# A parallel H3 convolution and ReLU FFN on one core: operand preparation in single steps, matmuls of the first classical product by high parts, a second half staged in row buffers, PSUM seeded by ScalarE, and longer pauses ahead of two convolution stages

## The chip, the cores and the metric

The kernel runs on one core of a Trainium2 chip. The time is device time in microseconds of one execution, median of several. The profile is of one further execution; its span runs from the first to the last instruction of the core.

## The reference

For `S = 2048` tokens and `D = 576` channels, with `xn` the rows of `x = A_q` after layer normalization:

```
k_shift = causal depthwise convolution of k with 4 taps (shift_k)
kv      = k_shift * v
y       = causal convolution of kv with ssm_k, over all 2048 positions, per channel   (FFT)
y       = y + kv * ssm_D
A       = xn * y
B       = relu(xn @ w1) @ w2           # w1: 576 x 4608, w2: 4608 x 576
out     = x + A + B
```

All is float32.

## The kernel before, in words

**FFN.** A float32 factor is split into a high part (rounded to fp32r) and a low part (the rest), and a product is three matmuls: high by high, high by low, low by high. The tokens are handled in two halves of 1024, the 4608 hidden units in 18 chunks of 256. A half with a chunk is a *quad*, `g` from 0 to 35. In a quad two token blocks `b` of 512 and two column blocks `f` of 128 make a 2 by 2 product. Quads 0 and 1 do it with four *classical* products (`classical`, 14 matmuls of 512 columns each). Quads 2 to 35 (`quad`) do it with seven products (`product`, six matmuls each) on the combined operands `00, 01, s2, s1, s3, s4, 11` and combined weights `wa, wb, wc, wd`, and four short `rest` products (`hl`, `wr`) for the last 64 of the 576 channels. The hidden sums stand in two PSUM banks that are used in turn (`psh`, tags h0 and h1). `hidden` ends a sum: ScalarE writes its ReLU as high part `hh`, VectorE the rest as low part `ll`, and only then is the bank free.

Between the products of quad `g` stand the eight *units* of quad `g - 1` (`mm2`: 12 matmuls of 288 columns, for 128 tokens): hidden units times `w2`, summed in a tile `pso` of PSUM, of which there are two. VectorE adds `pso` to the row tile `acc` (L656; L652 in the quads 0 and 1, with `rstd` as factor), which frees it. `split_w` splits weights, high parts on ScalarE (L444), low parts on GpSimd (L445), and GpSimd also issues the loads of the weights.

**Start.** Quads 0 and 1 work on centred rows that are not yet scaled by `rstd`. For quad 2 the scaled operands of blocks 0 and 1 are made by `scales` (a diagonal of `rstd`, `diag`, times a tile of ones on TensorE gives a row of factors, copied by ScalarE), `scaled` (VectorE multiplies `xf`), `combined` (differences for s1 to s4), `made` and `made_rest` (splits). The bottom of the function writes the calls in their order. The operands of the second half are made later, in `later_operands`: rows loaded, normalized, stored, transposed, combined, split into a tile `stg`, and stored to `ops_n`, from which quads 17 on load them.

**Convolution.** `conv` is a generator with the stages fb (`later_operands`), fk (first transform of the filter, `ks` and `zk`), fx (taps `tap`, `gate`, split `xs`, first transform `zx`), fm (`spectrum`, `product_of`, `way_back`) and fo (inverse transform, gate with `xn`, sum with the FFN). Each stage has its own tile pool, and the pools take over each other's memory. `tick(cost)` runs after each FFN piece, adds the piece's matmul columns to a clock, and draws the next step of `conv` when the clock times `rate` has paid for the weights (`W_FK`, `W_FX`, ...) of the steps drawn. A step that yields `-n * PAUSE` (16000 columns) stops the drawing until so many FFN columns have been issued: that is the lead time between a stage's loads and its first use. What a stage posts on VectorE and ScalarE stands behind the last `acc` and `hh` posted before it (`here`).

The order on each engine is then set by a list scheduler at build time (a model of the engines, which may move an instruction that depends on nothing ahead of or behind its place in the program). Each engine works through its list in order. SP issues the loads of `k`, `v`, `zt` and the rows, and the stores, in one queue; the loads of the weights and of the transform matrices stand in GpSimd's.

## Time and profile before

| | |
|---|---|
| time, median of 3 runs | 1096.8 us (1094.36 to 1098.38) |
| profiled execution | 1097.09 us, span 1095.0 us |
| TensorE (PE) busy | 1051.7 us, 96% |
| VectorE (DVE) busy | 769.9 us, 70% |
| ScalarE (ACT) busy | 485.5 us, 44% |
| GpSimd (POOL) busy | 457.8 us, 42% |
| granted TensorE clock, mean | 0.991 |

PE is the engine that is nearly always busy, so what can change the time is where it waits, and where its clock is lowered. The stages follow from the tiles at work: quads 0 and 1 to 62 us, quad 2 from 69 us, fb to about 285 us, fk to 425 us, fx to 700 us, fm from 743 to 975 us, fo to 1075 us.

### The profile page before, as it was taken

The page shows a single profiled execution, that of the slowest core. Times are in us where ns is not written, and L with a number is a line of the kernel's source. Part 1 is how long each engine was busy: PE and PEld are TensorE (multiplying, and loading weights), DVE is VectorE, ACT ScalarE, POOL GpSimd, SP SyncE. Part 2 cuts the span into 40 slices and gives each one's busy share as a digit, 9 for nine tenths or more (in the row PEclk, how much of TensorE's full clock was granted, in tenths as well). Part 3 has the DMA queues.
Part 4 walks back from the last instruction along what each step waited for, and adds up shares of the span by engine and source line. Part 5 has one row for each costly group of instructions (what it writes and reads, how often), then busy time and mean ns, then how long its engine had stood idle before and what let it go on. Part 6 is the DMA issues. An engine that isn't in the chain of part 4 may idle for free. (4 is left out here: it accounts for less than half of the span.)

```text
span 1095.0 us, 17070 instructions
## 1 busy us (share of the span) xinstructions
PE 1051.7 (96%) x6300; PEld 870.8 (80%) x6300; DVE 769.9 (70%) x1149; ACT 485.5 (44%) x929; POOL 457.8 (42%) x496
## 2 busy tenths in 40 slices
PE   8878999999999999798999999999999999999998
PEld 5766899999899998697899899895666665677777
DVE  5787768554887774999999999853444454446765
ACT  7342344333687774344444445434444444432220
POOL 3343454444354444454444445443223223244450
PEclk9989999999999999999999999999999999999999
DMA  6118544992254445589944433237566666457684
GB/s 166 58 38 187 144 150 183 197 154 56 89 160 139 140 140 160 153 259 349 279 134 138 137 114 120 78 138 194 174 197 208 189 209 203 131 179 223 220 248 119
DMA packets 118431, 179.45 MB, mean 164 GB/s; under 512 B 66381, under 2 KB 67551, under 8 KB 116556
## 3 DMA queue, kind: packets, MB, share of 16 engines
q1 hardware_dynamic: 99212, 121.99, 39.3%
q0 software_dynamic: 18816, 55.49, 17.0%
q10 hardware_dynamic: 320, 0.88, 0.3%
q8 instruction: 50, 0.82, 0.3%
q14 instruction: 33, 0.27, 0.1%
HBM read 123.27 MB, written 45.61 MB: 154 GB/s over the span
## 5 line engine op out<-in xcount | busy, mean ns | idle before, releaser
L501 PE MATMUL pso<-w,hh 128*128 128x288 f32 x2304 | 471.4, 297 | 5.4 <-DVE acc L652 3.3
L501 PEld LDWEIGHTS pso<-w,hh 128*128 128x128 f32 x2304 | 381.1, 189 | 36.2 <-issue 8.2
L501 PE MATMUL pso<-w,ll 128*128 128x288 f32 x1152 | 340.4, 295 | 0.0
L656 DVE TENSOR_TENSOR acc<-pso,acc 128x576 f32<-128x576 f32 x272 | 204.6, 753 | 158.0 <-PE pso L501 156.7
L501 PEld LDWEIGHTS pso<-w,ll 128*128 128x128 f32 x1152 | 217.1, 188 | 0.0
L445 POOL TENSOR_TENSOR w<-r,w 128x576 fp32r<-128x576 f32 x72 | 111.5, 1552 | 134.6 <-ACT w L444 134.5
L445 POOL TENSOR_TENSOR wb<-sums,wb 128x512 fp32r<-128x512 f32 x34 | 49.8, 1465 | 203.8 <-ACT wb L444 140.9
L501 PE MATMUL psh<-x,wa 128*128 128x512 f32 x408 | 109.0, 402 | 10.8 <-DVE ll L522 6.5
L501 PE MATMUL psh<-xs,wb 128*128 128x512 f32 x408 | 108.7, 400 | 1.2 <-ACT u L581 1.2
L501 PEld LDWEIGHTS psh<-x,wa 128*128 128x128 f32 x408 | 74.7, 190 | 32.6 <-issue 12.7
L501 PEld LDWEIGHTS psh<-xs,wb 128*128 128x128 f32 x408 | 72.9, 189 | 25.0 <-issue 11.7
L501 PE MATMUL psh<-hl,wr 128*128 128x512 f32 x272 | 88.1, 401 | 1.5 <-ACT psh L604 1.5
L521 ACT ACTIVATE hh<-psh 128x512 fp32r<-128x512 f32 x68 | 40.6, 598 | 91.0 <-PE psh L501 90.7
L604 ACT ACTIVATE psh<-psh 128x512 f32<-128x512 f32 x34 | 19.9, 584 | 132.7 <-DVE u L602 132.7
L445 POOL TENSOR_TENSOR wd<-r,wd 128x256 fp32r<-128x256 f32 x36 | 31.7, 881 | 97.1 <-ACT wd L444 97.1
L522 DVE SCALAR_TENSOR_TENSOR ll<-psh,hh 128x512 fp32r<-128x512 f32 x68 | 46.6, 685 | 34.1 <-ACT hh L521 33.7
L868 DVE TENSOR_TENSOR k<-psf,k 128x512 f32<-128x512 f32 x72 | 44.7, 682 | 36.5 <-PE psf L687 31.6
L676 DVE TENSOR_TENSOR ks<-kt,ks 64x288 fp32r<-64x288 f32 x64 | 54.5, 852 | 18.1 <-ACT ks L675 17.0
L445 POOL TENSOR_TENSOR wa<-r,wa 128x512 fp32r<-128x512 f32 x36 | 51.5, 1430 | 28.8 <-ACT wa L444 28.7
L501 PEld LDWEIGHTS psh<-hl,wr 128*128 128x128 f32 x272 | 46.9, 188 | 19.2 <-issue 12.3
L521 ACT ACTIVATE hh<-p 128x512 fp32r<-128x512 f32 x34 | 21.5, 632 | 90.4 <-DVE p L611 65.4
L501 PE MATMUL psh<-xs,wc 128*128 128x512 f32 x204 | 53.3, 396 | 8.1 <-DVE ll L522 8.1
(146 smaller groups left out, 1642.8 us busy)
## 6 DMA issues: line engine op xcount, KB each, us to landing
r<-in_w POOLq DMA_DIRECT2D x70, 288.0 KB, 3.5
r<-in_w POOLq DMA_DIRECT2D x35, 512.0 KB, 5.2
zk<-zk SPq DMA_DIRECT2D x32, 288.0 KB, 2.6
zx<-zx SPq DMA_DIRECT2D x32, 288.0 KB, 2.7
ztk<-zk SPq DMA_DIRECT2D x18, 512.0 KB, 3.9
ztx<-zx SPq DMA_DIRECT2D x18, 512.0 KB, 3.9
k<-k SPq DMA_DIRECT2D x72, 128.0 KB, 3.2
zy<-vo SPq DMA_DIRECT2D x18, 512.0 KB, 2.6
```

Of the source, the lines that this page charges most:

```text
L445: nc.gpsimd.tensor_tensor(w[:, 1, :n], src, w[:, 0, :n], OP.subtract)
L501: last = nc.tensor.matmul(ps, a, m, start=start and n == 0, stop=n == len(seq) - 1, skip_group_check=True)
L521: done["act"] = nc.scalar.activation(hh, ps, AF.Relu)
L522: nc.vector.scalar_tensor_tensor(ll, ps, 0.0, hh, op0=OP.max, op1=OP.subtract)
L604: nc.scalar.activation(x, y, AF.Copy, scale=-1.0)
L656: done["acc"] = nc.vector.tensor_tensor(two(acc[t]), ps[:, :, :NH], two(acc[t]), OP.add)
L676: nc.vector.tensor_tensor(dst[other], src[own], dst[own], OP.subtract)
L868: nc.vector.tensor_tensor(filt[n][c][:, k, :], banks[k], filt[n][c][:, k, :], OP.mult)
```

## The change

It changes these parts (names as in the code; a `PAUSE` is 16000 columns):

- `classical`: with `g == f == 0` the eight matmuls on the operands' high parts stand first, the four on their low parts after them. Before, high and low parts alternated.
- The start: both diagonals are made before the units; `scales(1)` and `scales(0)` have matmuls between them and the diagonals. The operands of quad 2 are made by a generator, `second_half_of_start`, one chunk a step; `post` draws steps after units and classical products, `need` draws until an operand that is asked for is ready. Units and products of quad 1 stand in another order, quad 2 is issued within the pool `fa`, and the convolution begins with quad 3.
- `quad`: unit 3 stands ahead of the product with s1, and unit 4 ahead of the product with s3; before, they stood behind these.
- Seeds: while `stage["seeded"]` is (3, 4), which is from the opening of the pool of fx to that of fm, units 3 and 4 have ScalarE copy `acc` into `pso` (`open_unit`), the matmuls add to it, and ScalarE copies `pso` back to `acc`. VectorE's sum falls away for them. There are 26 such units.
- `later_operands`: all four row tiles are loaded at once (four buffers, before three), and the tile `stg` is replaced by the row buffers, with two stores of 512 KB an operand instead of one of 1 MB.
- The four loads of `sk` move from SP's queue to GpSimd's.
- Pacing: the pause between the loads and the first step of fx is 4 (before 2.5), the steps up to its first transform pause 2.375 (before 1.125); in fm the pause is 3.5 (before 1.5). `KT_GAP`, `PAUSES`, `SHARE`, `FFN_TOTAL` and the weights `W_...` take other values.

Three places show how instructions move. VectorE, from the first low part of operand 00 (`x00`) to the end of the third sum of quad 1 (`ll1_1_0`), whose bank takes the first product of quad 2; before:

```order
L207 TENSOR_TENSOR x00_622<-xf00_227,x00_622 128x512 x2
L207 TENSOR_TENSOR x01_627<-xf01_229,x01_627 128x512 x2
L203 TENSOR_TENSOR hl0_632<-xfr0_231,hl0_632 64x512
L457 TENSOR_TENSOR sums2_662<-r1_2_420 128x256 x2
L221 TENSOR_TENSOR xf10_335<-xf10_335,xf00_227 128x512 x2
L207 TENSOR_TENSOR xs1_567<-xfs1_564,xs1_567 128x512
L313 TENSOR_TENSOR xfr1_339<-xfr1_339,row1_558 64x512
L207 TENSOR_TENSOR xs1_567<-xfs1_564,xs1_567 128x512
L207 TENSOR_TENSOR xs2_635<-xfs2_619,xs2_635 128x512 x2
L522 SCALAR_TENSOR_TENSOR ll1_1_0_656<-psh1_c10_640,hh1_1_0_655 128x512
```

and now:

```order
L207 TENSOR_TENSOR x00_614<-xf00_227,x00_614 128x512 x2
L221 TENSOR_TENSOR xfs2_646<-xf00_227,xfs1_583 128x512
L508 TENSOR_TENSOR sums2_651<-r1_2_420 128x256 x2
L221 TENSOR_TENSOR xfs2_646<-xf00_227,xfs1_583 128x512
L508 TENSOR_TENSOR sums2_651<-sums2_651,r1_2_420 128x256
L575 SCALAR_TENSOR_TENSOR ll1_1_0_635<-psh1_c10_619,hh1_1_0_634 128x512
```

Twelve operations stood between; now five do, two of them the combination of s2, which stood ahead of `x00` before. The rest now stands behind `ll1_1_0`.

VectorE, the making of block 1's rest operand `hl1`, which the `rest` behind unit 6 of quad 1 reads in quad 2; before:

```order
L522 SCALAR_TENSOR_TENSOR ll1_1_1_686<-psh1_c11_670,hh1_1_1_685 128x512
L207 TENSOR_TENSOR x11_713<-xf11_337,x11_713 128x512 x2
L207 TENSOR_TENSOR xs3_701<-xf10_335,xs3_701 128x512 x2
L203 TENSOR_TENSOR hl1_719<-xfr1_339,hl1_719 64x512
L207 TENSOR_TENSOR xs4_708<-xf01_229,xs4_708 128x512
```

and now:

```order
L726 SCALAR_TENSOR_TENSOR acc4_111<-pso1_5_814,rstd_84,acc4_111 128x576
L315 TENSOR_TENSOR xfr1_339<-xfr1_339,row1_464 64x512
L575 SCALAR_TENSOR_TENSOR ll2_0_1_861<-u2_2_785,hh2_0_1_860 128x512
L726 SCALAR_TENSOR_TENSOR acc6_118<-pso1_6_864,rstd_84,acc6_118 128x576
L207 TENSOR_TENSOR x11_899<-xf11_337,x11_899 128x512 x2
L203 TENSOR_TENSOR hl1_879<-xfr1_339,hl1_879 64x512
L676 TENSOR_TENSOR p5_2_809<-psh2_2_698,p5_2_809 128x512
```

It stood ahead of all units of quad 1, and now stands behind the sum of unit 6 (`acc6_118<-pso1_6`) and two low parts.

VectorE, the first tap of fx, `c0<-k0,sk`, which needs the first loads of that stage; before (psh15 and ll15 are quad 15, pso14 its units):

```order
L602 TENSOR_TENSOR u2_15_4520<-psh15_5_4522,u2_15_4520 128x512
L656 TENSOR_TENSOR acc4_111<-pso14_5_4570,acc4_111 128x576
L769 TENSOR_TENSOR c0_4481<-k0_4259,sk_4258 128x576
L522 SCALAR_TENSOR_TENSOR ll15_0_1_4603<-u2_15_4520,hh15_0_1_4602 128x512
L656 TENSOR_TENSOR acc6_118<-pso14_6_4606,acc6_118 128x576
L611 TENSOR_TENSOR p5_15_4532<-psh15_2_4438,p5_15_4532 128x512
L656 TENSOR_TENSOR acc6_118<-pso14_7_4625,acc6_118 128x576
L772 TENSOR_TENSOR e0_1_4506<-k-1_4268,sk_4258 128x576
```

and now:

```order
L676 TENSOR_TENSOR p5_15_4564<-psh15_2_4454,p5_15_4564 128x512
L833 MEMSET k-1_4210 1x576
L833 MEMSET k-2_4215 1x576
L833 MEMSET k-3_4220 1x576
L730 TENSOR_TENSOR acc6_118<-pso14_7_4635,acc6_118 128x576
L575 SCALAR_TENSOR_TENSOR ll15_1_1_4656<-p5_15_4564,hh15_1_1_4655 128x512
L575 SCALAR_TENSOR_TENSOR ll15_1_0_4694<-psh15_4_4611,hh15_1_0_4693 128x512
L844 TENSOR_TENSOR c0_4502<-k0_4201,sk_4200 128x576
L730 TENSOR_TENSOR acc0_100<-pso15_0_4699,acc0_100 128x576
L847 TENSOR_TENSOR e0_1_4534<-k-1_4210,sk_4200 128x576
```

The tap stood ahead of the last three low parts `ll` of quad 15 and now stands behind them. TensorE's last matmul of fk moved too, from behind unit 3 to behind unit 5 of that row of units.

The diff, cut:

```diff
-PAUSES = 19
-SHARE = 0.99
+PAUSES = 22.5
+SHARE = 0.983
...
-W_FK, W_FX, W_FMK, W_FMX, W_FMB, W_FO = 2.5, 5.8, 2.4, 4.8, 3.4, 6.6
+W_FK, W_FX, W_FMK, W_FMX, W_FMB, W_FO = 2.3, 6.4, 3.8, 3.8, 2.6, 6.0
-KT_GAP = 6000
-N_FB, W_FB = 37, 3.9
+KT_GAP = 4500
+N_FB, W_FB = 37, 4.0
...
+    def second_half_of_start(pool):
+        for o, b in (("11", 1), ("10", 1), ("00", 0), ("01", 0), (0, 0)):
+            yield from scaled(o, b)
+        yield from combined(pool, "s1")
+        yield "00"
+        yield from made("00")
+        yield from made("01")
+        yield from made_rest(0)
+        yield from combined(pool, "s2")
+        yield from made("s2")
+        yield from made("s1")
+        yield from combined(pool, "s3")
+        yield from made("s3")
+        yield from combined(pool, "s4")
+        yield "10"
+        yield from made("s4")
+        yield from scaled(1, 1)
+        yield from made_rest(1)
+        yield from made("11")
...
+    def need(g, o):
+        while g == PLAIN and o not in ready:
+            post(1)
...
-        for t in range(first, first + 6, 2):
+        for t in range(first, T, 2):
             load_rows(t)
...
-            dst = pool.tile([P, 2, 2, 512], F32R, tag="stg", name=f"stg{o}")
...
+                raw = pool.tile([P, 2, D], F32, tag="xn", name=f"stg{o}{c}", bufs=4)
+                dst = raw[:, :, :512]
...
+                nc.sync.dma_start(ops_n[o][:, :, c, :], dst)
                 yield W_FB
-            nc.sync.dma_start(ops_n[o], dst.bitcast(F32))
...
+                if firsts:
+                    firsts.insert(-1, (h, hi))
+                    firsts.append((l, hi))
+                else:
+                    firsts = [(h, hi), (l, hi)]
+                lasts.append((h, lo))
+        if g == f == 0:
+            seq, late = firsts + lasts, []
...
         nc.scalar.activation(u2, y, AF.Copy)
+        unit(3)
         x = bank(g, 0, "5")
...
-        unit(3)
-        product(y, wb[g], 2, "s3")
+        unit(4)
+        product(y, wb[g], 2, "s3", g=g)
...
-        unit(4)
         rest(x, g, b0, 1)
...
+        if seed:
+            seeded.add(t)
+            nc.scalar.activation(ps[:, :, :NH], two(acc[t]), AF.Copy)
...
-            matmuls(ps[:, h, :NH], seq, True)
-        if g < PLAIN:
+            matmuls(ps[:, h, :NH], seq, t not in seeded)
+        if t in seeded:
+            done["act"] = nc.scalar.activation(two(acc[t]), ps[:, :, :NH], AF.Copy)
+            seeded.remove(t)
+        elif g < PLAIN:
...
+            stage["seeded"] = (3, 4)
...
-                    nc.sync.dma_start(sk[:, -t, :], shift_k[-t:1 - t, :].to_broadcast([P, D]))
+                    nc.gpsimd.dma_start(sk[:, -t, :], shift_k[-t:1 - t, :].to_broadcast([P, D]))
...
-            yield -2.5 * PAUSE
+            yield -4 * PAUSE
...
-            yield -1.5 * PAUSE
+            yield -3.5 * PAUSE
             spectrum(0)
...
+        diag = [diagonal(fa, b) for b in range(2)]
+        unit(0, 0)
+        unit(0, 1)
+        scales(fa, 1, diag[1])
         classical(1, 0, 0, 0, 0)
...
+        scales(fa, 0, diag[0])
+        posts["at"] = second_half_of_start(fa)
+        unit(0, 2)
+        post(1)
+        unit(0, 3)
+        post(1)
+        classical(1, 0, 1, 1, 0, "00")
...
+        for i in range(BT):
+            unit(1, i)
+            post(2, "10")
+        classical(1, 1, 0, 0, 0, "10")
...
+        classical(1, 1, 1, 1, 0, "10")
...
+        quad(PLAIN, [(PLAIN - 1, b, i) for b in range(2) for i in range(BT)])
+        post(99)
     clock["until"] = clock["ffn"]

-    for g in range(PLAIN, QUADS):
+    for g in range(PLAIN + 1, QUADS):
```

130 lines of the change are left out of this document (66 added, 64 removed).

## The prediction, made before the changed kernel was run

> **What bounds the kernel now.** I read the page's table of engines first, then the list of what PE waited for, in two stretches and for the rest, then the timeline around the longest waits.
>
> ```profile
> PE 1051.7 (96%) x6300; PEld 870.8 (80%) x6300; DVE 769.9 (70%) x1149; ACT 485.5 (44%) x929; POOL 457.8 (42%) x496
> ```
>
> PE is busy 1051.7 of 1095 us, and the change leaves its matmuls as they are. So it can win what PE waits, and what PE loses to a lowered clock after a wait. From 30 to 127 us (quads 0 to 3) PE waited for
>
> ```profile
> PE psh L501 <- DVE ll L522: 7.3, 2, 6.5
> PE psf L302 <- DVE diag L298: 3.4, 2, 1.7
> PE pso L501 <- DVE acc L652: 3.3, 4, 1.1
> PE psh L501 <- ACT psh L566: 1.6, 1, 1.6
> PE psh L501 <- ACT u L581: 0.7, 1, 0.7
> ```
>
> (us in total, times, longest), 16.3 us together, and from 425 to 710 us (the entry of fx, and fx) for
>
> ```profile
> PE psh L501 <- DVE ll L522: 7.4, 4, 3.6
> PE psh L501 <- DVE p L611: 2.7, 1, 2.7
> PE pso L501 <- DVE acc L656: 2.0, 3, 1.2
> PE psh L501 <- ACT psh L604: 1.5, 1, 1.5
> PE psf L682 <- DVE xs L676: 1.0, 1, 1.0
> ```
>
> 14.6 us together. Behind 710 us there are 3.3 us. Nearly all of it is waiting for VectorE (or for a ScalarE copy of what VectorE made). Three of the waits leave a low clock behind, in the stretches that follow them:
>
> ```profile
> 68.80:72.00 3.20, 3.20 (x9) 2.62 (x10) 3.20 (x7) 2.02 (x4) 0.89 (x1) 0.53 0.00 0
> 439.50:444.00 4.50, 4.48 (x17) 4.06 (x18) 4.48 (x6) 2.31 (x6) 3.13 (x4) 0.62 1.04 225
> 498.40:502.00 3.60, 3.60 (x15) 3.31 (x15) 3.60 (x6) 0.60 (x2) 0.42 (x1) 0.53 1.09 312
> ```
>
> The third number from the end is the granted clock: 0.53, 0.62 and 0.53 of full speed over 3.2, 4.5 and 3.6 us lose 3.2 x 0.47 + 4.5 x 0.38 + 3.6 x 0.47 = 1.5 + 1.7 + 1.7 us. That makes 17.8 us at the start and 18.0 us in fx that a better order could win, 35.8 us in all.
>
> **The start: what goes.** The two rows of factors cost PE a wait each, since the diagonal stands behind the sum of a unit on VectorE:
>
> ```profile
> 38.17 0.87 DVE L298 TENSOR_SCALAR diag<-ident,rstd 128x128 f32<-128x128 f32 x4
> 39.09 1.12 PE L302 MATMUL psf<-diag,ones 128*128 128x512 f32 x2 [1.69 <-DVE diag L298]
> ```
>
> Made right behind `rstd`, both diagonals (2 x 0.87) are ready by 33.3 us, before PE ends the second unit: 3.4 us go, hidden behind two units. The longest wait is the first product of quad 2, whose bank is freed by `ll1_1_0`:
>
> ```profile
> 67.98 0.67 DVE L522 SCALAR_TENSOR_TENSOR ll<-psh_c,hh 128x512 fp32r<-128x512 f32 x1
> 68.80 2.90 PE L501 MATMUL psh<-x,wa 128*128 128x512 f32 x6 [6.55 <-DVE ll L522]
> ```
>
> VectorE was some 7 us behind there. I followed the new order by hand with the rows' durations (0.82 a sum, 0.62 from start to start of a 128x512 operation, and for PE
>
> ```profile
> 1019.82 1.85 PE psh L501 x8
> 1059.53 1.59 PE pso L501 x12
> ```
>
> 0.23 us a 512-column matmul and 1.59 us a unit). PE ended quad 1 some 6.6 us before 68.80, at 62.1; without the waits for `diag` it does at 58.7. The third sum of quad 1 ends 14 x 0.23 = 3.2 us before, `hh` takes 0.6, and VectorE comes to `ll1_1_0` at 57.0, done at 57.6. So this wait goes, and with it the waits for `acc` L652 (3.3 us), which came from VectorE standing at `bn` for rows that had not landed:
>
> ```profile
> 84.85 1.54 DVE L172 BATCH_NORM_STATS2 bn<-xn 128x6 f32<-128x288 f32 x4 [4.81 <-DMA xn<-in_x]
> ```
>
> These now come a quad later, with all loads issued at once and 16000 columns (7 us) ahead. I take all 17.8 us as gone.
>
> **The start: what comes.** (a) On VectorE `ll0_0_1` now stands ahead of the centring of block 1's third tile, so that tile waits for the end of the second classical product: it is done at about 22.2 instead of 21.55 us, 0.5 us. (b) The low part of `wa2` on GpSimd comes 0.7 us after the product that reads it. (c) `hl1` stands behind the sum of unit 6: PE ends unit 6, goes on to the `rest` with `hl1`, and VectorE still has the sum and two low parts ahead of it:
>
> ```profile
> L652 DVE SCALAR_TENSOR_TENSOR acc<-pso,rstd,acc 128x576 f32<-128x576 f32 x16 | 12.9, 809 | 5.0 <-PE pso L501 5.0
> L207 DVE TENSOR_TENSOR x<-xf,x 128x512 fp32r<-128x512 f32 x6 | 3.8, 680 | 0.0
> L203 DVE TENSOR_TENSOR hl<-xfr,hl 64x512 fp32r<-64x512 f32 x2 | 2.4, 1177 | 0.1
> ```
>
> 0.8 + 2 x 0.62 + 0.7 to 1.2, about 2.9 us of a new wait, after which the clock may fall: 0.8 us, the middle of 0 and 1.7. (d) Small waits on VectorE in quad 3, 0.5 us. Together 5.4 us, so the start wins 12.4 us.
>
> The Trainium skill (TensorE: Matmul & The Clock Gate, "What's actually happening") puts the clock at half only after an idle window of about 3.4 us; by that the 2.9 us of (c) cost no clock and the sum is 0.8 us less. The trace disagrees: the 0.53 behind 498.4 us follows a wait of 1.5 us, so I keep the middle.
>
> **The first classical product.** It waits for the operand's low part:
>
> ```profile
> 14.00 2.73 PE L501 MATMUL psh_c<-x,wa 128*128 128x512 f32 x10 [0.71 <-DVE x L277]
> 15.77 0.68 DVE L278 TENSOR_TENSOR hl<-psf,hl 64x512 fp32r<-64x512 f32 x1
> ```
>
> With the low parts last this wait is covered, but the product then ends with the low part of `hl`, which VectorE has at 16.45 us, 0.15 us before PE asked for it. It ends at 16.45 + 2 x 0.23 = 16.9 where it ended at 17.4: 0.4 us are won.
>
> **Fx: the entry.** In the trace the tap waits for its loads and holds up the rest of quad 15:
>
> ```profile
> 436.84 0.76 DVE L769 TENSOR_TENSOR c<-k,sk 128x576 f32<-128x576 f32 x1 [4.68 <-DMA k<-in_k]
> 439.52 2.14 PE L501 MATMUL psh<-x,wa 128*128 128x512 f32 x6 [2.65 <-DVE p L611]
> 455.81 1.66 PE L501 MATMUL psh<-xs,wc 128*128 128x512 f32 x6 [3.57 <-DVE ll L522]
> ```
>
> The longer pause does not appear in the order: from fk's last matmul to the tap there were a product, a `rest`, another product and two units (6.4 us), now two units, two `rest` and a product (5.5 us) and the two steps of `ll`. So the loads, which wait for fk's memory, are hardly further ahead. What differs is who stands behind the tap: now `acc0` of quad 15's units, which PE needs two units and two products later, some 6 us. The `sk` load no longer shares SP's queue:
>
> ```profile
> DMA to landing us min/median/max: 5.0/7.5/8.2
> r<-in_w POOLq DMA_DIRECT2D x70, 288.0 KB, 3.5
> ```
>
> (the four loads of `sk`, and loads of the same size from GpSimd's queue), so it may land 4 us sooner. A wait of up to 5 us on VectorE is then covered; without that cover PE would pay it in full.
>
> The Trainium skill (DMA: Bandwidth & Descriptors, "Specifications") has GpSimd's path slower to the first byte, 1 us against 0.6 us. By that `sk` lands 0.4 us later and not sooner, 0.4 us more; the rows above say otherwise, if GpSimd's queue is free.
>
> **Fx: the rest.** VectorE is full there:
>
> ```profile
> 450.00:700.00 250.00, 240.49 (x1447) 218.02 (x1445) 243.71 (x314) 113.54 (x227) 122.19 (x124) 0.99 0.58 179
> L656 DVE TENSOR_TENSOR acc<-pso,acc 128x576 f32<-128x576 f32 x73 | 54.5, 749 | 2.7 <-PE pso L501 2.3
> ```
>
> 243.7 of 250 us (the third number), ScalarE 113.5. Seeds take two of eight sums, 18 x 0.749 = 13.6 us of VectorE's 243.7, and give ScalarE two copies each. No seed is in the trace; the nearest row of that size is a copy on ScalarE:
>
> ```profile
> L444 ACT ACTIVATE w<-r 128x576 fp32r<-128x576 f32 x72 | 48.2, 678 | 0.2
> ```
>
> 0.68, so about 0.7 us each way and 18 x 1.4 = 25 us, to 139 of 250: room enough. Moving unit 3 gives `ll` of the first sum 1.59 us more before its bank is asked for, which covers all but the 3.57 of the four waits for `ll`. Remaining: in the first two quads of fx VectorE has some 31 us of work for a quad of 25 us (20 operations of the taps at about 0.95, four `xs` at 1.13, six sums, the quad's own; start to start 0.07 us less each):
>
> ```profile
> L772 DVE TENSOR_TENSOR e<-k,sk 128x576 f32<-128x576 f32 x42 | 42.4, 1009 | 0.1
> L676 DVE TENSOR_TENSOR xs<-c,xs 64x576 fp32r<-64x576 f32 x30 | 33.9, 1131 | 1.9 <-ACT xs L675 1.0
> ```
>
> So waits for u, p and `acc` stay: I take 5 us, 1 us later in the stage and 1 us of clock, 7 of the 18. The bounds are 0 (all goes) and 18 (VectorE stays as late). So fx wins 11 us.
>
> **Fm and fo.** The pause ahead of fm buys nothing, since its loads were issued 26 us before the first use at 743 us:
>
> ```profile
> 716.63 0.80 SPq L833 DMA_DIRECT2D ztk<-zk x2
> ```
>
> At its start two groups now stand only three matmuls (0.7 us) apart, while ScalarE's four copies of a group take 4 x 0.6 us less overlap:
>
> ```profile
> L853 ACT ACTIVATE k<-psf 128x512 f32<-128x512 f32 x72 | 37.3, 603 | 27.2 <-PE psf L687 27.2
> L878 ACT ACTIVATE vo<-psf 128x512 f32<-128x512 f32 x36 | 19.6, 596 | 49.1 <-issue 29.7 <-PE psf L687 18.1 <-ACT wb L444 0.8
> ```
>
> About 0.9 us. Fm is drawn over fewer columns (254 against 290 thousand), and in four places only 0.5 to 0.7 us of matmuls stand between a way back and the next group, against two copies `vo` of 1.1 us: 4 x 0.4 us. Together 2.5 us lost; bounds 0 and 8 (18 groups of products at 0.45). Fk, fo and the end I cost at nothing: fo's loads are issued three steps ahead, and in fk both engines have a quarter to spare,
>
> ```profile
> 285.00:425.00 140.00, 139.46 (x861) 127.86 (x860) 107.59 (x152) 104.35 (x200) 67.97 (x78) 1.00 0.42 138
> ```
>
> (VectorE 107.59 and ScalarE 104.35 of 140 us).
>
> **The sum.** 1097.1 - 12.4 - 0.4 - 11 + 2.5 = 1075.8 us against the profiled execution, which is 0.3 us over the median of the runs: **1076 us**, 1.9% faster.
>
> **The rivals.**
> - *Nothing left to wait for* (0.14): neither `hl1` nor the entry of fx costs anything, as GpSimd's and VectorE's rows at the start have much idle time. 1097.1 - 35.8 + 2.5 + 1 = 1065 us. Against it: `hl1`'s place in the order is plain.
> - *Fx keeps its waits* (0.18): the lead to the tap is not longer, VectorE's 31 us a quad remain, and 13.6 us of relief in 250 are eaten by catching up. 1097.1 - 12.8 + 2.5 = 1087 us; with 5 us more in the start or in fm it ends at 1092, no change.
> - *Seeds queue on ScalarE* (0.08), the case on the other side. A seed waits for the bank of the unit two places before, freed by VectorE; ScalarE's queue stands meanwhile, with the copies u2, p5 and y behind it, and PE waits for them. For it: sums were late enough to stop PE three times in fx, by up to 1.2 us. Against it: PE takes 4.9 us from unit 1 to unit 3 (two products, a `rest`, a unit). It decides from the point where sums are over 4 us late; then each of 26 seeds costs its 0.7 us and about as much for the copies behind it, 26 x 1.4 = 36 us, with no gain in fx: 1097.1 - 12.8 + 2.5 + 36 = 1123 us; half of the quads, 1105.
>
> **How the numbers follow.** The forecast, from 1066 to 1085 us by its own bounds, has 0.60. The range 1064 to 1089 us reaches to the first two rivals and leaves out the third and the worst of the second. A measurement of this kernel tells about 0.5% from no change (1091.3 to 1102.3 us): faster 0.60 + 0.14 + 0.13, same 0.05 of the second rival and 0.03 of the third, slower 0.05.
>
> **What would show it.** Right: no wait for `diag` and none over 1.5 us at quad 2's first product; one of about 3 us at the `rest` with `hl1`; the tap's wait on DMA still there, with no PE wait for p behind it; VectorE at 90 to 94% in fx; PE waits of 6 us from 425 to 710. Wrong: new waits of ScalarE at the seed lines and of PE for them, waits of PE for `k` or `vo` throughout fm, or waits in fk, where for two quads the seeds meet a ScalarE that is already 75% busy.

## The result: 1090.6 us, and where the time went

| | before | changed |
|---|---|---|
| time, median (lowest to highest) | 1096.8 us (1094.36 to 1098.38) | 1090.62 us (1088.99 to 1091.25) |
| ratio, 95% interval | | 0.9945 (0.9928 to 0.9962) |
| span of the profiled execution | 1095.0 us | 1089.4 us |

The change makes the kernel 0.55% faster, where 1.9% was forecast. The page of the changed kernel, engines:

```profile
PE 1052.9 (97%) x6300; PEld 873.7 (80%) x6300; DVE 752.8 (69%) x1123; ACT 516.1 (47%) x981; POOL 462.1 (42%) x500
```

PE is busy as long as before (1051.7), VectorE 17 us less, ScalarE 31 us more: the seeds moved work from VectorE to ScalarE, as they were meant to. What PE waited for from 30 to 127 us (us in total, times, longest):

```profile
PE psh L552 <- DVE hl L203: 4.2, 1, 4.2
PE pso L552 <- DVE acc L726: 1.2, 1, 1.2
PE psh L552 <- POOL wa L496: 1.2, 1, 1.2
PE psf L307 <- DVE diag L299: 0.6, 1, 0.6
```

7.2 us, where it was 16.3. From 425 to 710 us it waited for

```profile
PE pso L552 <- DVE acc L730: 6.7, 2, 6.4
PE psh L552 <- ACT psh L669: 3.2, 2, 2.7
PE psf L756 <- DVE xs L750: 2.4, 3, 1.1
```

and 2.4 us in three others: 14.7 us, where it was 14.6. Other operations are waited for, and the sum is the same.

**Stage by stage.** Matmuls of the FFN move from one stage to the next when the order changes, so stages can't be compared by their times alone. I cut the profiled executions at PE's 240,000th column of matmuls (at 135 to 150 us), at the last matmul with `wk`, at the last with `wx` and at the last of all, and took from the time between two cuts 0.4455 ns for each column issued there (512 columns take 0.228 us from start to start). What is left is waiting, low clock and the pipeline's own losses, and it can be compared. The rows of the cuts, of before and of the changed kernel (min/median/max ns, first to last start):

```profile
L682 PEld LDWEIGHTS psf<-ks,wk x128: 186/188/189, 281.8 to 424.3; 128*128 128x128 f32 x128
L682 PEld LDWEIGHTS psf<-xs,wx x128: 186/188/191, 460.8 to 713.2; 128*128 128x128 f32 x128
```
```profile
L756 PEld LDWEIGHTS psf<-ks,wk x128: 186/188/191, 284.8 to 426.4; 128*128 128x128 f32 x128
L756 PEld LDWEIGHTS psf<-xs,wx x128: 186/188/331, 459.7 to 720.9; 128*128 128x128 f32 x128
```

Difference to the kernel before, in us, by that account (this table serves the experiments below; their names are explained there):

| kernel | start | to the end of fk | fx | fm, fo, end | sum |
|---|---|---|---|---|---|
| *predicted* | -12.8 | 0 | -11 | +2.5 | -21.3 |
| changed | -8.1 | +3.8 | +1.8 | -3.4 | -5.9 |
| hl1_early | -10.4 | +3.7 | +0.1 | -3.2 | -9.8 |
| w_split_late | -4.3 | +5.4 | +0.9 | -3.0 | -1.0 |
| sk_on_sp | -6.7 | +3.8 | -2.7 | -3.2 | -8.8 |
| no_seeds | -8.0 | +1.8 | +2.1 | -3.5 | -7.6 |
| fm_as_before | -8.4 | +2.7 | +5.5 | +1.6 | +1.4 |
| units_back | -6.3 | +5.1 | +4.2 | -0.1 | +2.9 |
| before_units_moved | -1.7 | +0.5 | -1.6 | -2.4 | -5.2 |
| lead_9 | -8.4 | +4.2 | -6.2 | -2.6 | -13.0 |
| lead_9_late_seeds | -8.7 | +1.0 | -6.6 | -2.5 | -16.8 |
| lead_9_no_seeds | -8.4 | +1.0 | -11.8 | -2.6 | -21.8 |
| lead_9_no_seeds_hl1 | -10.1 | +0.9 | -9.4 | -2.6 | -21.2 |
| lead_8_no_seeds_hl1 | -10.0 | +0.9 | -4.3 | -4.2 | -17.6 |
| lead_11_no_seeds_hl1 | -10.1 | -0.1 | -0.7 | +3.4 | -7.4 |
| before_lead_9 | +4.0 | +5.7 | +0.4 | -4.9 | +5.2 |
| old_second_half | -6.4 | +3.6 | +10.8 | -2.8 | +5.3 |

It is made from one profiled execution of each kernel; the medians of the runs stand with each experiment. The start won 8.1 of the 12.8 us that were forecast. Fk lost where nothing was expected, and fx, which was to give 11 us, lost 1.8. Fm won where a loss was expected, which hides 5.9 us of the miss.

**The entry of fx** is the main part of the miss. The timeline there, and PE's clock (the third number from the end) in the stretches in which it was low:

```profile
436.26 1.22 DVE L844 TENSOR_TENSOR c<-k,sk 128x576 f32<-128x576 f32 x1 [2.09 <-DMA k<-in_k]
443.81 0.76 DVE L847 TENSOR_TENSOR e<-k-1_4210,sk 128x576 f32<-128x576 f32 x1 [5.67 <-DMA k-1_4210<-in_k]
445.30 0.85 PE L552 MATMUL pso<-w,hh 128*128 128x288 f32 x2 [6.44 <-DVE acc L730]
```
```profile
445.30:448.98 3.68, 3.68 (x14) 3.58 (x15) 1.70 (x3) 0.00 (x0) 0.00 (x0) 0.50 1.03 244
466.05:469.46 3.41, 3.41 (x13) 3.08 (x12) 3.41 (x4) 0.14 (x1) 1.01 (x1) 0.50 0.52 167
479.70:483.12 3.42, 3.42 (x11) 2.85 (x10) 2.88 (x6) 1.23 (x4) 0.00 (x0) 0.50 0.62 158
```

The first two taps now wait for their loads, 2.09 and 5.67 us, and the second wait stands ahead of the second sum of quad 15, whose bank PE needs: PE waits 6.44 us. Behind this wait and two later ones the clock is at half, which costs half of 3.68 + 3.41 + 3.42 us, 5.3 us by 484 us.

### The profile page after: what moved, and what is told of

It is laid out like the page before. It is cut to its first block, busy times and chain, and to the rows that moved or that the text cites. A ratio compares the mean times of both kernels' runs of the same rounds, so it can differ in the third digit from the quotient of the medians.

```text
span 1089.4 us, 17144 instructions
## 1 busy us (share of the span) xinstructions
PE 1052.9 (97%) x6300; PEld 873.7 (80%) x6300; DVE 752.8 (69%) x1123; ACT 516.1 (47%) x981; POOL 462.1 (42%) x500
## 4 chain that ended last, share of the span: by engine, by line
PE 78%; DVE 12%; DMA 4%; issue 3%; ACT 3%; SPq 0%; POOL 0%; DVEq 0%; ACTq 0%; POOLq 0%
PE pso L552 35%; PE psh L552 31%; PE psf L761 8%; PE psf L756 2%; DVE ll L575 2%; DVE c L848 2%; DMA acc<-in_x 2%; DVE acc L730 1%; DVE e L847 1%; DVE xs L750 1%; DMA k<-in_k 1%; PE psh_c L552 1%; DMA v<-in_v 1%; DVE sums L508 1%; DVE c L853 1%
## 5 line engine op out<-in xcount | busy, mean ns | idle before, releaser
L730 DVE TENSOR_TENSOR acc<-pso,acc 128x576 f32<-128x576 f32 x246 | 185.0, 754 | 143.3 <-PE pso L552 141.3
L496 POOL TENSOR_TENSOR wd<-r,wd 128x256 fp32r<-128x256 f32 x36 | 34.0, 945 | 93.8 <-ACT wd L495 93.8
L552 PE MATMUL psh<-x,wc 128*128 128x512 f32 x204 | 55.9, 406 | 0.0
```

The source lines that it names most:

```text
L496: nc.gpsimd.tensor_tensor(w[:, 1, :n], src, w[:, 0, :n], OP.subtract)
L552: last = nc.tensor.matmul(ps, a, m, start=start and n == 0, stop=n == len(seq) - 1, skip_group_check=True)
L730: done["acc"] = nc.vector.tensor_tensor(two(acc[t]), ps[:, :, :NH], two(acc[t]), OP.add)
```

## Experiments

All are edits of the changed kernel, but for the two whose names begin with before. All times are medians; before ran in 1095.5 to 1096.1 us beside them. An edit of one number also moves instructions in the scheduler's order, often in other stages, so no experiment here changes one thing alone; where the order matters, the text says how it moved.

### The start: hl1 and GpSimd

*hl1_early.* Edit:

```diff
-        for o, b in (("11", 1), ("10", 1), ("00", 0), ("01", 0), (0, 0)):
+        for o, b in (("11", 1), ("10", 1), ("00", 0), ("01", 0), (0, 0), (1, 1)):
             yield from scaled(o, b)
 ...
         yield from made("s4")
-        yield from scaled(1, 1)
         yield from made_rest(1)
```

> The changed kernel with the two steps that make hl1 earlier in the start's second half: its scaling among the first five, its split right behind s4 and ahead of 11 (on VectorE between the sums of units 5 and 6 instead of behind the sum of unit 6 and two low parts of 11). The profile after has a wait of 4.2 us of PE for hl at 88 us and a clock of 0.50 and 0.75 for 4 us each behind it, 7 us together. Theory A (only hl1's place in VectorE's order costs this): the wait falls under 1 us, no low clock, 1083 to 1086 us. Rival (VectorE is behind all through quad 2, and the next product waits instead): 3 us or more of new waits from 60 to 127 us, 1087 to 1091 us.

Measured: 1089.08 us (ratio to before 0.9938, 0.9923 to 0.9953), the rival's time. The wait for `hl` fell to 0.6 us and the low clock at 88 us is gone, as theory A had it, but from 30 to 127 us PE waited 5.4 us, with 1.0 for `xs` and 0.6 for `u` that it had not waited for, and in the profiled execution the clock was at half from 23 us (see the last section), 1.7 us. Of 7 us the start kept 2.3. In two other kernels below the same edit gave 2.7 and 1.1 us.

*w_split_late.* Edit: the loop with `split_w2(0, j)` and `load_w2(1, j)` goes behind `classical(0, 1, 0, 1, 0)`.

> The changed kernel with the split of w2's first two tiles behind block 1's first classical product instead of ahead of it, so that GpSimd does not work while VectorE centres block 1's third tile. In the profile after, this one operation took 1.73 us beside GpSimd's 128x576 operation, where it took 0.52 before the change, and PE waited 2.0 us for it. Theory A (VectorE is slowed by GpSimd's elementwise work beside it): the centring takes 0.6 us or less, PE's wait for it falls below 1.2 us, and the time by about 1 us unless unit 0 waits for its weights. Rival (it is slow for another reason): 1.7 us as before.

Measured: 1095.12 us (0.9994, 0.9982 to 1.0005). The timeline of the changed kernel, then of this one:

```profile
21.34 1.73 DVE L239 TENSOR_SCALAR xn<-acc,mv 128x576 f32<-128x576 f32 x1
21.35 2.99 POOL L496 TENSOR_TENSOR w<-r,w 128x576 fp32r<-128x576 f32 x2 [2.15 <-ACT w L495]
```
```profile
21.72 0.51 DVE L239 TENSOR_SCALAR xn<-acc,mv 128x576 f32<-128x576 f32 x1
34.15 2.93 DVE L299 TENSOR_SCALAR diag<-ident,rstd 128x128 f32<-128x128 f32 x3
34.32 0.75 POOL L496 TENSOR_TENSOR wr<-r,wr 128x256 fp32r<-128x256 f32 x1
...
PE psf L307 <- DVE diag L299: 3.3, 1, 3.3
PE psx L226 <- DVE xn L239: 1.3, 2, 0.8
```

Without GpSimd beside it the centring takes 0.51 us, and PE's longest wait for it falls from 2.0 to 0.8: the cause is shown. But GpSimd now works beside `diag`, three of which take 2.93 us (in the kernel before four took 0.87), PE waits 3.3 us there, and the clock is 0.79 for 8 us behind it. The collision was moved to a worse place, and the 1 us that theory A hoped for became a loss of 4.5.

### The entry of fx

*sk_on_sp.* Edit:

```diff
-                    nc.gpsimd.dma_start(sk[:, -t, :], shift_k[-t:1 - t, :].to_broadcast([P, D]))
+                    nc.sync.dma_start(sk[:, -t, :], shift_k[-t:1 - t, :].to_broadcast([P, D]))
```

> The changed kernel with the four loads of sk back on SyncE's queue. In the profile after, GpSimd's queue (sk, wx, weights) took 63 to 67% of the 16 DMA engines from 434 to 446 us and SyncE's, with the rows that the taps wait for next, 37 to 48%; before, SyncE's queue took 71 to 105%. Theory A (the share of the queues makes the rows of k late): the rows of k-1 land within 11.5 us of the first k load's issue instead of 13.4, PE's wait of 6.4 us at the entry of fx falls below 4, and the time to 1085 to 1089 us. Rival (both queues share one bandwidth, so only the total counts): wait and time as in the changed kernel, 1089 to 1092 us.

Measured: 1087.20 us (0.9917, 0.9902 to 0.9932), 3.4 us under the changed kernel and as theory A had it. What the queues moved from 438 to 442 us (packets, MB, share of the 16 engines; q0 is GpSimd's, q1 SyncE's), in the changed kernel and in this one:

```profile
q0 software_dynamic: 215, 0.66, 63.1%
q1 hardware_dynamic: 225, 0.43, 48.1%
```
```profile
q1 hardware_dynamic: 521, 1.02, 100.0%
q0 software_dynamic: 11, 0.05, 5.4%
```

The engines are full either way. With `sk` on GpSimd's queue, `sk`, `wx` and the weights there take more than half of them while the rows of `k` wait on SyncE's. With `sk` on SyncE's queue, the tap on k-1 started 10.4 us behind the issue of the first `k` load (13.4 in the changed kernel), and PE's longest wait was 3.3 us. But VectorE's order changed as well:

```profile
439.76 1.42 DVE L730 TENSOR_TENSOR acc<-pso,acc 128x576 f32<-128x576 f32 x2
442.63 1.84 DVE L847 TENSOR_TENSOR e<-k-1_4210,sk 128x576 f32<-128x576 f32 x1 [1.45 <-DMA k-1_4210<-in_k]
```

The second sum of quad 15 (first row) now stands ahead of the second tap, so PE no longer waits for it behind a load. The earlier landing is shown; how much of the 3.4 us is the queue's and how much the order's is not.

*lead_9.* Edit: `yield -4 * PAUSE` becomes `yield -9 * PAUSE`, `PAUSES` 27.5.

> The changed kernel with a pause of 9 instead of 4 ahead of fx's first tap (the total of pauses raised by as much): on VectorE the first tap then stands behind ll of quad 16 and three sums of quad 15 that stood behind it. Theory A (the tap is issued ahead of its loads and what stands behind it stops PE): the wait of 6.4 us, the low clock behind it and part of the waits to 480 us go, 1080 to 1085 us. Rival (VectorE has too much to do in the first two quads of fx wherever they start): waits of the same sum appear later, 1088 to 1091 us.

Measured: 1084.35 us (0.9894, 0.9879 to 0.9909), as theory A had it. On VectorE the first tap now stands behind three more sums and a low part, and PE's waits from 425 to 500 us, 12.0 us in the changed kernel, are two, of 2.0 and 0.6 us:

```profile
440.64 0.76 DVE L730 TENSOR_TENSOR acc<-pso,acc 128x576 f32<-128x576 f32 x1 [0.27 <-PE pso L552]
441.32 1.03 DVE L844 TENSOR_TENSOR c<-k,sk 128x576 f32<-128x576 f32 x1
443.26 0.76 DVE L847 TENSOR_TENSOR e<-k-1_4106,sk 128x576 f32<-128x576 f32 x1 [0.92 <-DMA k-1_4106<-in_k]
...
PE psh L552 <- ACT p L652: 2.0, 1, 2.0
```

By the table fx is 8 us shorter than in the changed kernel, and the other stages are within 1 us of it. The change's own pause, 4 instead of 2.5, had left the first tap ahead of all the sums of quad 15 and the second tap behind only one of them.

*fm_as_before.* Edit: the pause ahead of fm 1.5 again, `W_FMK, W_FMX, W_FMB` 2.4, 4.8, 3.4, `PAUSES` 20.5.

> The changed kernel with the pause ahead of fm (1.5) and the three weights of fm's pieces as before, the total of pauses lowered by as much. By stages, fm took 3.1 us less than before the change, where the prediction had it 2.5 us slower. Theory A (the longer pause gives the loads and the first filter time, and PE's wait of 2.5 us at 753 us went for it): 1092 to 1094 us with a wait of 2 to 3 us at the start of fm. Rival (the longer pause and the weights do nothing; units 3 and 4 did it, since with them in their old places fm took 3.3 us more): 1089 to 1091.5 us.

Measured: 1096.57 us (1.0003, 0.9992 to 1.0013), slower than either expectation. Fm is 5.0 us longer, with PE's wait at its start back (second row; the first is at the entry of fx):

```profile
PE psh L552 <- ACT psh L669: 10.4, 1, 10.4
...
PE psf L761 <- issue: 1.8, 1, 1.8
```

So the pause and the weights of fm do win in the changed kernel. They are not the only way: *before_units_moved* (below) has the old pause and no such wait, and *units_back* has the new pause and a wait of 1.9 us there. At the entry of fx, the total of pauses sets the pace of all stages: the taps fell ahead of another operation of the quad (`u`, which ScalarE copies), and PE waited 10.4 us. The edit in fm moved the entry of fx.

*before_lead_9.* The kernel before, with the pause 9 instead of 2.5 (`PAUSES` 25.5).

> The kernel before with one number changed: 9 instead of 2.5 for the pause ahead of fx's taps (total of pauses raised by as much). On VectorE the first tap then stands behind two ll and three sums that stood behind it. Theory A (the entry of fx stalls in the kernel before for the same reason, 2.65 + 1.3 + 3.6 us of waits and 1.7 us of clock): 1088 to 1091 us. Rival (in the kernel before, waits for ll and p come from the order of the units, and the taps' place does not matter): 1095 to 1098 us.

Measured: 1100.41 us (1.0043, 1.0028 to 1.0058), slower than even the rival's range. At the entry (425 to 500 us) PE's waits fell from 9.4 to 1.8 us, so the taps were the cause there as well; but from 500 to 730 us it waited 12.0 us, most of it 5.0 and 2.7 for `y` and `ll`, and fx was as long as before. The start and fk got longer too, by the new pace.

### The seeds

*no_seeds.* Edit: `stage["seeded"] = ()` in fx.

> The changed kernel with no unit seeded: VectorE makes all sums again (the order then has the first tap behind two more sums). Theory A (the seeds give VectorE the 13 us in fx that the prediction counted on, and PE waits less for it): behind 500 us PE's waits rise from some 4 us to 10 to 14, VectorE's share from 500 to 710 us from 92% to 96%, and the time is 1093 to 1098 us unless the entry gains. Rival (the seeds bring nothing in fx and the burst of copies in fk and at the entry costs): waits behind 500 us stay under 5 us, the entry loses its 6.4 us wait, and the time is 1083 to 1088 us.

Measured: 1090.24 us (0.9948, 0.9931 to 0.9965): the same as with seeds. Neither expectation held: behind 500 us PE was busy 3.8 us less, in fk and at the entry it lost less (the order had changed there too). That asked for the comparison with the entry out of the way:

*lead_9_late_seeds* sets `stage["seeded"]` only ahead of fx's loop; *lead_9_no_seeds* never does; both with the pause of 9.

> The kernel with the pause of 9, and seeds only from fx's first matmuls on, none in fk and at the entry of fx. Counted by stages (the time from stage to stage less 0.4455 ns a column), fk lost 3.5 us to before with seeds and 1.5 without, and from 500 to 710 us PE was busy 207.4 us with seeds and 203.6 without. Theory A (seeds cost in fk, where ScalarE is busy, and win in fx): 2 us less in fk and fx as with the pause of 9, 1081 to 1083 us. Rival (seeds are worth nothing either way, it is the scheduler's order that differs): 1084 to 1087 us.

> The kernel with the pause of 9 and no unit seeded; in VectorE's order the entry of fx is the same as in the one with the pause of 9 and late seeds, so the two differ only by the seeds behind fx's first matmuls. Theory A (a seed takes a sum of 0.75 us from VectorE, which is full in fx, and late seeds are worth what the profiles show behind 500 us, 4 us): 1084 to 1086 us against 1080.8, and 3 to 5 us more of PE's waits in fx. Rival (seeds are worth nothing): 1080 to 1082 us.

Measured: 1084.35 with all seeds, 1080.83 with late ones (0.9864, 0.9849 to 0.9879), 1075.49 with none (0.9820, 0.9805 to 0.9834). Seeds cost 8.9 us, 3.5 of them in fk and at the entry. For the step from late seeds to none neither theory had the sign. The engines from 500 to 710 us, with late seeds and with none (behind the length of the stretch come PE's busy time, its weight loads', then VectorE's and ScalarE's):

```profile
500.00:710.00 210.00, 203.83 (x1229) 185.21 (x1228) 195.66 (x247) 112.96 (x221) 104.91 (x106) 0.99 0.50 146
```
```profile
500.00:710.00 210.00, 206.68 (x1257) 187.98 (x1256) 205.81 (x271) 99.42 (x197) 109.16 (x107) 1.00 0.50 146
```

Without seeds VectorE is busy 98% of the time instead of 93%, and PE waits less. In the changed kernel, what ScalarE stood idle for ahead of its 26 seeds (us, times):

```profile
L704 ACT ACTIVATE pso<-acc x26: 636/656/662, 382.2 to 723.7; 128x576 f32<-128x576 f32 x26
...
  DVE acc L730: 24.5, 18
```

In 18 of 26 cases ScalarE's queue stood for a sum of VectorE, 24.5 us in all, and what stood behind the seed in that queue waited as well.

*lead_9_seeds_own_bank.* Edit, on the kernel with late seeds: `tag=f"o{t % 2}", bufs=1` for `pso`, and likewise for the start's tiles.

> The kernel with the pause of 9 and late seeds (1080.8 us), with the two banks of the sums given to units by turns (even and odd), so that a seed can't take the bank that the unit ahead of it waits for. In that kernel's trace the seed of the fourth unit stood right behind the sum of the first (571.8 us), so it sat in the first unit's bank, and the third unit began only behind the sum of the second (573.3 us, a wait of 2.25). Theory A (this swap is what the seeds cost): 1074 to 1077 us, the waits of PE for acc at such places under 1 us. Rival (a seed costs by its place in ScalarE's queue and by its own 0.7 us ahead of the unit): 1079 to 1082 us.

Measured: 1080.47 us (0.9856, 0.9838 to 0.9874), no gain. Waits from 500 to 730 us with late seeds, then with banks by turns:

```profile
PE pso L552 <- DVE acc L730: 3.8, 3, 2.3
PE psf L756 <- DVE xs L750: 1.5, 2, 1.2
PE psh L552 <- ACT psh L669: 0.8, 1, 0.8
```
```profile
PE psh L552 <- ACT psh L669: 2.7, 4, 0.9
PE pso L552 <- DVE acc L730: 1.8, 2, 0.9
PE psf L756 <- DVE xs L750: 0.9, 1, 0.9
PE pso L552 <- ACT pso L704: 0.7, 1, 0.7
```

The longest wait is gone, so the swap of banks was there; the sum is the same 6.1 us, now for copies of ScalarE. This speaks for ScalarE's queue, but no run changes the queue alone. Of the 5.3 us between late seeds and none, the waits of PE explain 2.8 (6.1 against 3.3 from 500 to 730 us), and a low clock behind the wait of 2.3 us, which the kernel without seeds does not have, 1.7 more:

```profile
573.95:577.35 3.40, 3.40 (x14) 3.12 (x13) 2.04 (x4) 1.68 (x3) 1.75 (x2) 0.50 0.33 93
```

### The places of units 3 and 4

*units_back* puts them back in the changed kernel; *before_units_moved* moves them in the kernel before and changes nothing else.

```diff
+        unit(3)
         x = bank(g, 0, "5")
 ...
-        unit(3)
+        unit(4)
         product(y, wb[g], 2, "s3")
 ...
-        unit(4)
         rest(x, g, b0, 1)
```

> The changed kernel with units 3 and 4 of a quad back in their old places (3 behind s1, 4 behind s3). Theory A (the unit between s2 and s1 covers ll, so that PE's waits for ll in fx, 7.4 us before, are gone for this reason): PE's waits for ll return, 4 us or more from 425 to 710 us, and the time rises to 1094 to 1097 us. Rival (the seeds or the pacing did it): waits for ll under 2 us and a time within 3 us of the changed kernel's.

> The kernel before with one edit of the change alone: units 3 and 4 in their new places. Put back in the changed kernel, the old places cost 9 us. Theory A (the move wins by itself, since it covers ll and the copies that wait for it): 1088 to 1092 us, waits for ll at most 8 us (the 6.5 at quad 2 stays). Rival (the move wins only with the rest of the change): 1095 us or more, the entry of fx waiting as long in other places.

Measured: 1099.55 us without the move (1.0035, 1.0023 to 1.0048), and 1091.73 us with the move alone (0.9960, 0.9945 to 0.9976). This one edit takes 3.7 us off the kernel before, where the whole change takes 6.2, and without it the change is a loss. Undone, it costs in every stage: 1.8, 1.3, 2.4 and 3.3 us by the table. Theory A of units_back named the wrong wait: those for `ll` came back to 0.7 us only; in fx those for `acc` (9.2 us) and `p` (1.6) grew, and in fk those for `y`'s copy (2.7).

*old_second_half.* Pauses, weights, KT_GAP, places of units 3 and 4, queue of `sk` and plain sums as before, in the changed kernel.

> The changed kernel with the second half's pauses and weights, the places of units 3 and 4, the queue of sk and the plain sums as before: what is left of the change is the start (and the staging in the rows' buffers). By the waits of the profile the new start wins some 8 us and the second half of the change gives some 2 back (PE's clock at the entry of fx, 3 us of waits in fk; against them 2 us at the start of fm). Theory A (the second half of the change brought nothing): 1087 to 1090 us, not slower than the changed kernel's 1090.6. Rival (the second half did win, and the start won less than its waits say): 1093 us or more.

Measured: 1105.72 us (1.0086, 1.0069 to 1.0104). This is outside both ranges. The new start with the old pace is a loss: fx is 10.8 us longer than before, and fo runs to the end of the FFN (last matmul of fo at 1089 us of 1095; 1070 of 1084 in the changed kernel). The pace counts the FFN's work from the end of the start, which now lies a quad later, so this kernel isn't the start by itself, and the first expectation overlooked that.

### All together

*lead_9_late_seeds_hl1*, *all_four* (the same with `sk` on SyncE's queue), *lead_9_no_seeds_hl1*, *lead_8_no_seeds_hl1*, *lead_11_no_seeds_hl1*: the edits above in one kernel, the last two with a pause of 8 and 11.

> The kernel with the pause of 9, late seeds, and hl1 made earlier. Theory A (the three losses lie in different stages and add up): 1.5 to 4 us under the 1080.8 without the edit to hl1, 1077 to 1079.5 us. Rival (the earlier end of the start is eaten at the entry of fx by the loads): 1080 to 1082 us.

> The kernel with the pause of 9, late seeds, hl1 made earlier, and the loads of sk on SyncE's queue. Theory A (the share of the queues still matters with the later tap): 1 to 3 us under the same kernel with sk on GpSimd's queue. Rival (with the tap later, its loads have landed, and the queue does not matter): within 1 us of it.

> The kernel with the pause of 9, no seeds and hl1 made earlier. Without hl1's edit it ran in 1075.5 us; with late seeds the edit gave 2.7 us. Theory A (the gains add up): 1072 to 1074 us. Rival: the entry of fx takes it back, 1075 to 1076 us.

> The kernel with no seeds and hl1 made earlier, at a pause of 8 instead of 9 (1074.4 us) or 11 (1087.5): the first tap stands at the same place of VectorE's order as with 9, the others one or two operations earlier. Theory A (a broad optimum around 9; at 11 the stages behind are squeezed): 1073 to 1077 us. Rival (single orders of instructions decide, and any change of the pause moves the time by several us): 1079 us or more.

> The same with a pause of 11: the first tap then stands behind all of quad 15's first seven sums. Theory A (at 9 the loads have landed when the taps come; the rest of fx is squeezed together by a longer pause): 1 to 5 us slower than with 9. Rival (the taps still come too early at 9): 1 to 2 us faster.

| kernel | us | ratio to before, 95% |
|---|---|---|
| lead_9_late_seeds_hl1 | 1078.17 | 0.9846 (0.9831 to 0.9860) |
| all_four | 1079.40 | 0.9854 (0.9839 to 0.9868) |
| lead_9_no_seeds_hl1 | 1074.43 | 0.9806 (0.9789 to 0.9823) |
| lead_8_no_seeds_hl1 | 1079.74 | 0.9845 (0.9823 to 0.9867) |
| lead_11_no_seeds_hl1 | 1087.53 | 0.9927 (0.9911 to 0.9944) |

The queue of `sk` gains nothing once the taps come later (1.2 us slower, inside the intervals). The best kernel is 1.9% faster than before and 1.5% faster than the changed one: the change with a longer pause, without seeds, and with `hl1` earlier. It is no broad optimum: one step of the pause down costs 5 us and two steps up 13, though on VectorE the first tap stands at the same place with 8 as with 9 and the next ones one or two operations earlier. At 11 PE waited twice 2.7 us for `ll` in the middle of fx and 2.3 us at the start of fm. So single orders decide some 5 us here, and a difference of 1 to 2 us between two such kernels says little of the edit.

## Why the prediction was wrong, point by point

The sum missed by 15 us: fx came out 12.8 us worse than forecast, the start 4.7 and fk 3.8, and fm 5.9 better. The step that failed most is the one from "VectorE is full there" to 11 us won in fx.

- **What bounds the kernel** (right): PE's busy time stayed, and what was won or lost is waits, nearly all on VectorE and on ScalarE's copies, and the clock behind them.
- **The start, what goes** (right): 17.8 us were taken as gone. Of the waits for `ll` none is left, of those for `diag` 0.6 us (five of its eight operations took 2.54 us beside GpSimd, where four took 0.87 before).
- **The start, what comes** (terms mis-sized): (a) 0.5 us for the centring, measured 2.0, since it took 1.73 us beside GpSimd; (b) 0.7 us for `wa`, measured 1.2; (c) 2.9 us for `hl1`, measured 4.2, since a low part took 1.77 us instead of 0.68 (below), and the clock behind it, at half from 88.17 to 94 us, lost 2.9 us and not 0.8. (a) to (c) were forecast at 4.9 us and measured at 10.3; the start won 8.1 instead of 12.8, the first classical product included.
- **The clock behind waits** (mis-sized in (c)): the granted clock was 0.50 behind the wait of 4.25 us, and 0.61 from 480 to 484 us behind two waits of 1.0 and 1.4 us. The Trainium skill (TensorE: Matmul & The Clock Gate, "What's actually happening") puts the clock at half behind an idle window of some 3.4 us. The wait of 4.25 us agrees with it in length; the two of 1.0 and 1.4 us are together too short to hold such a window, so there the measurement differs from the page, as the prediction had it, and it decides.
- **The first classical product** (right in size): 0.4 us forecast. PE's waits for low parts of `x`, 0.7 us in the first product of each of the two blocks, are gone; 0.5 us for `hl` and `xf` came, together.
- **Fx: the entry** (wrong in the step "what differs is who stands behind the tap ... some 6 us", and in "it may land 4 us sooner"). Only the first tap's wait was weighed (up to 5 us, covered); it was 2.09. The second tap's, for k-1, was not in the sum: 5.67 us, ahead of the second sum. lead_9 puts both taps behind quad 15's first sums, and fx is 8 us shorter. And with `sk` on GpSimd's queue the rows of k-1 came later, 13.4 us behind the first load and not 10.4: while the 16 DMA engines were full, GpSimd's queue took 63% of them. The median landing of `sk` itself did not fall by 4 us: it was 7.7 us on GpSimd's queue and 7.5 before. By the first-byte figures of the Trainium skill (DMA: Bandwidth & Descriptors, "Specifications") GpSimd's path is 0.4 us slower, an estimate; the trace agrees in sign, and it is small beside the 3 us.
- **Fx: the rest** (wrong in the step from busy time to waits): "VectorE is full there", so 13.6 us less for it should be worth most of the stage's waits. VectorE did fall to 92% (193.1 of the 210 us from 500 on, before 201.6), inside the 90 to 94% that the prediction named. Yet with the pause of 9 and no seeds, at 98%, PE waited less and the kernel was 5 to 9 us faster. What PE waits for is the order of a few operations at a few places, not the sum of busy time; a seed adds two copies to ScalarE's order, and the first of them has to wait for VectorE.
- **The move of units 3 and 4** (right in kind, mis-sized): credited with covering three of four waits for `ll`, a share of 11 us in fx; alone it is worth 3.7 us over all stages.
- **Fk and fm**: fk was costed at nothing ("both engines have a quarter to spare") and lost 3.5 us. The list of what would show the forecast wrong had this case; counted from its first matmul, fk lost 1.6 us without seeds, and 0.2 with late ones and the pause of 9, so most of it is the seeds' price. In fm, "the pause ahead of fm buys nothing" was wrong: the loads of `zt` were early, but by the order of the rows PE's wait of 2.5 us came from the transfers that swap the first filter's halves, which VectorE awaited:

```profile
754.94 2.54 DVE L868 TENSOR_TENSOR k<-psf,k 128x512 f32<-128x512 f32 x4 [4.93 <-DMA k<-k]
756.38 1.08 PE L687 MATMUL psf<-ztk,m_sb 64*64 64x512 f32 x4 [2.51 <-issue]
```

(the kernel before; PE went on 0.1 us behind the second of VectorE's four operations, though the profile names no releaser). With the longer pause and the new weights this wait is gone, and fm_as_before brings it back, but so does units_back. So fm's gain hangs on the order at this place, to which both edits add. The losses of 2.5 us forecast in fm did not come: from 710 us on PE waited 1.2 us, before 3.3.
- **The range and the rivals.** The sum's own bounds reach further than the range: with all 18 us kept in fx and 8 us lost in fm it is 1075.8 + 11 + 5.5 = 1092 us, and not 1085 or 1089. The rival "Fx keeps its waits" (1087 us, up to 1092) came true in its time and in fx, and had 0.18, too little. Of its reasons the entry of fx is shown by lead_9; that VectorE's relief would be eaten by catching up is not what happened, since VectorE fell to 92%. The mechanism of "Seeds queue on ScalarE" was there too, at some 9 us with the pause of 9 and not 36: it is no longer hidden once the entry is mended.

## What to carry to other kernels

An engine at 98% need not hold up the one that matters, and taking work from it need not help: ask which operation stands ahead of which at the few places where the bound engine waits, and give one more cover there, as the move of two units did. A transfer's consumer should stand in its engine's queue behind all that is ready earlier; if a pause is meant to do that, look whether the order changed. When several edits share a pace or an engine, test each with the others both in and out: the seeds were worth nothing in the change and cost 9 us once another loss was gone.

## What the runs showed of the hardware

**A VectorE operation can stand still while one of GpSimd runs.** With GpSimd's operation running, this low part took 1.77 us, where its kind takes 0.68 alone:

```profile
83.23 1.70 POOL L496 TENSOR_TENSOR wb<-sums,wb 128x512 fp32r<-128x512 f32 x1 [3.99 <-ACT wb L495]
83.70 1.77 DVE L575 SCALAR_TENSOR_TENSOR ll<-u,hh 128x512 fp32r<-128x512 f32 x1
```

GpSimd ended at 84.93, VectorE 0.54 us later: by these times it had waited for the rest of GpSimd's operation. The Trainium skill (SBUF — State Buffer, "Who interferes with whom") says so: VectorE with two inputs in SBUF, or in a fast mode, and GpSimd share one pair of ports, held for a whole instruction. The trace agrees here, in the centring (1.73 us for 0.52) and in `diag`, and w_split_late shows it for the centring by taking GpSimd away (0.51). The prediction's (a) and (c) should have carried it.

**Full DMA engines are divided between the queues.** From 434 to 446 us they moved 264 GB/s in the changed kernel, GpSimd's queue with 63 to 67% of them and SyncE's with 37 to 48%, though SyncE's had the rows that the taps waited for. In sk_on_sp SyncE's had 100% from 438 to 442 us, while GpSimd's was nearly empty, and about half in the 4 us ahead and behind, when both were in use.

**The granted clock can fall in one execution and not in another.** The changed kernel and lead_9 have the same instructions up to there and the same wait of 2.0 us at 21 us; the stretch behind it, in the one and the other:

```profile
24.00:28.00 4.00, 3.64 (x16) 2.18 (x14) 2.71 (x5) 3.69 (x7) 1.38 (x3) 1.00 0.46 147
```
```profile
24.00:28.00 4.00, 3.64 (x11) 2.49 (x10) 2.85 (x5) 3.83 (x7) 1.23 (x3) 0.60 0.43 147
```

Of the 16 kernels with this start and this wait, 11 show the low clock behind it and 5 do not. In all the traces here the clock is either 1.00 or 0.50, and each stretch at 0.50 ahead of the last matmul lasts 3.41 us or a multiple of it; in lead_9:

```profile
24.82:28.23 3.41, 3.41 (x8) 2.49 (x9) 3.08 (x5) 3.24 (x6) 0.41 (x1) 0.50 0.51 173
```

So such a drop costs 1.7 us where PE is busy all through it, and whether it comes behind a wait of 2 us differs from run to run: a term for it can only be a mean.
